# A single-core RWKV and MLP kernel: later landing times in its planner, second-batch loads held behind weight loads, and wide idle products

## The chip, the cores and the metric

The kernel runs on one core of one Trainium2 chip. The metric is device time in microseconds; lower is better. Each figure for a kernel is the median of several executions.

## The reference

The inputs are float64 in the kernel's reading (it loads pairs of 32-bit words and makes float32 of them). Per batch (4), a linear attention with decay over 768 positions, 8 heads of 48 columns:

```python
for t in range(S):
    kt, vt, rt = (k[:, :, t], v[:, :, t], r[:, :, t])
    cur = np.einsum('bhd,bhe->bhde', u[None] * kt, vt)
    y[:, :, t] = np.einsum('bhd,bhde->bhe', rt, state + cur)
    state = w[None, :, :, None] * state + np.einsum('bhd,bhe->bhde', kt, vt)
```

Its heads side by side are x (768 x 384 per batch), and then comes a gate of low rank over positions and an MLP:

```python
h = xt @ U @ V                                # U is 768 x 32, V is 32 x 768
u = x + h.transpose(0, 2, 1)
ch = np.maximum(u @ w_ch1, 0.0) @ w_ch2       # 384 -> 1536 -> 384
return (u + ch).astype(np.float32)
```

## The kernel before, in words

**Tiling.** A batch has 6 chunks of 128 positions; chunk n belongs to batch n // 6, and the chunks of the first batch are the "front" ones. For each chunk the kernel loads r, k and v (`a_load`, L630; tiles ld, or ldr, ldk and ldv) and the odd heads' v with its halves exchanged (`a_load_odd`, L661; vsw). From chunk 9 on (the second half of the second batch) r and k come as blocks of 32 rows (`a_load_blocks`, L674; bl), 32 transfers for three chunks, and DVE transposes them. A chunk's attention is done in two halves (`a_part`, L864). Each half is a run of small products on quarters of TensorE's array: pav (L824 and L830) is what the chunk gives, pab (L788 and L803) is the scores and state of the next chunk. Between the two halves a one-element copy, `seen` (L903), reads the first half's result, and the second half waits for it. After a half follow on DVE: the masking of the scores (am, L922), the state (S, L950) and, after the second half, x (L929).

**Gate and MLP.** For the first batch, x of each chunk is multiplied with U by `c_gx` (L972) into the bank `wake`; `c_g0` splits the sum (Gs). `c_x` turns x into the bank pu, `c_xu` adds the gate there and splits the result into a high and a low half (uTh, uTl). `m_1` and `m_2` are the MLP's products (p, through the helper at L344): w1 and w2 come in 12 pieces each and are also split into high and low halves (w1s, w2s). The first batch's MLP goes through its first 384 positions with half of the pieces, then through its second 384 with all, and then through the other half for the first.

**Weights.** `unit` (L492) makes a pair of steps for each of U, V and the 24 pieces: a load (L515; raw_u, raw_v, raw_w) and a conversion (L536 or L540, L562, L543, L546, then the splits at L580 and L581). No more than three pieces of w1 and w2 are under way: the load of one waits, by a dependency added by hand, for the landing of the third before it. `landing` lists these loads in their order, each with a buffer `landed_...` that stands for the landing in the plan; no tile is ever made of that buffer. The pieces' loads are taken in the order of their use.

**The planner.** All steps are first given to `Plan.op` with an engine, an estimated time, and what they read and write. `Plan.schedule` (L146) then simulates the engines and writes an order for each: at each moment it takes, among the steps that could start, the one with the smallest key (the steps' keys are the times given to `at`). The chip runs this order, each engine its own queue in turn, with semaphores only where tiles depend on each other. So an estimate changes the order and nothing else. For a DMA the plan takes a time in the queue, `LANDS` (1650 ns) and `late`; the loads of U, V and the weights have `late=LATE`, 400 ns. Where a step is ready in the plan before its data are on the chip, everything behind it on that engine's queue waits.

**The planned clock and the idle products.** The plan has a model of TensorE's clock, in windows of 3413 ns: a window runs at full speed if the window before it had work for over 0.36 of it, and at half otherwise (`clock`, L113). `pe_end` (L119) works out when a product ends and books its work. Where the plan finds TensorE idle between two given steps (`plan.wakes`, L1357), it fills the time with idle products, which nothing reads: up to the last product of `c_gx` one of the identity with itself (`waking`, L404; float32, 128 x 128, into the first 128 columns of `wake`, whose other 384 columns take `c_gx`'s sums), and later, until the first batch's first uTl is complete, `refill` (L1261), a product of V3 with V3.

## Time and profile before

| | |
|---|---|
| device time, median of 3 runs (lowest to highest) | 426.91 us (425.38 to 427.21) |
| the profiled execution's own time | 427.98 us |
| its span | 426.3 us |
| TensorE busy | 415.6 us, 98% |
| VectorE busy | 264.5 us, 62% |
| ScalarE busy | 137.3 us, 32% |
| GpSimd busy | 63.6 us, 15% |
| TensorE's granted clock, mean | 0.991 |
| DMA, mean over the span | 102 GB/s |

The span is the part of the execution that the profile shows; the profiled execution took 1.7 us more than it. Rows of the page name a line of the kernel, the engine, the operation and the tiles (out<-in). PE is TensorE, PEld its weight loads, DVE VectorE, ACT ScalarE, POOL GpSimd, and SPq and ACTq are the queues in which SyncE and ScalarE issue transfers. The slices show the whole run, 10.7 us a digit, in tenths busy and tenths of full clock:

```profile
PE   8998999999999999999999999999999999999994
DVE  6888897599999838676785466576622452113122
PEclk9998899999999999999999999999999999999999
```

TensorE is busy throughout. The first five slices hold the attention of the first batch with idle products between; from there on the MLP of each batch runs on TensorE with the attention of the next batch among it.

### The profile page before, as it was taken

What the parts mean: (1) busy time and instruction counts of PE and PEld (TensorE: products, weight loads), DVE (VectorE), ACT (ScalarE), POOL (GpSimd) and SP (SyncE); (2) the same over time, 40 slices, a digit from 0 to 9 for tenths busy, and PEclk for the clock granted to TensorE, in tenths of its full rate; (3) what the DMA queues carried; (4) which work ended last, traced back from release to release, by engine and by line L of the source; (5) the groups of instructions that cost most, each with busy time, mean ns of one, the idle gap of its engine ahead of it and who ended that gap; (6) DMA issues with size and microseconds to landing.
All of it is one profiled execution on the core that took longest, in us unless ns stands there. A gap on an engine that the chain in (4) does not pass through costs nothing.

```text
span 426.3 us, 12170 instructions
## 1 busy us (share of the span) xinstructions
PE 415.6 (98%) x5122; PEld 397.3 (93%) x5122; DVE 264.5 (62%) x598; ACT 137.3 (32%) x374; POOL 63.6 (15%) x100
## 2 busy tenths in 40 slices
PE   8998999999999999999999999999999999999994
PEld 8888899999999999999999999999999999999994
DVE  6888897599999838676785466576622452113122
ACT  2876695276541314112112221322112221111110
POOL 2654220053521003011100001101100000000000
PEclk9998899999999999999999999999999999999999
DMA  9979977697458676755477664231100420001001
GB/s 144 157 148 246 250 177 147 158 260 179 83 85 180 113 162 102 139 90 84 104 147 118 104 153 60 47 66 31 57 2 2 75 92 2 0 0 58 0 2 62
DMA packets 181951, 43.53 MB, mean 102 GB/s; under 512 B 168961, under 2 KB 180354, under 8 KB 181890
## 3 DMA queue, kind: packets, MB, share of 16 engines
q1 hardware_dynamic: 176706, 41.21, 48.2%
q10 hardware_dynamic: 5184, 1.48, 1.9%
q8 instruction: 42, 0.69, 0.7%
q14 instruction: 19, 0.16, 0.1%
HBM read 36.18 MB, written 6.49 MB: 100 GB/s over the span
## 4 chain that ended last, share of the span: by engine, by line
PE 84%; DMA 5%; SPq 5%; DVE 2%; ACT 1%; issue 1%; DVEq 0%; ACTq 0%
PE p L344 72%; SPq L655 4%; PE pav L824 4%; DMA raw_w<-in_moe_w_ch_dram 3%; PE pav L830 3%; PE pab L788 2%; PE pu L344 1%; DMA ub<-in_u_dram 1%; PE pab L803 1%; SPq L515 1%; DMA wT<-in_w_dram 1%; PE pG L995 1%; SPq L667 1%; DMA raw_v<-in_moe_V_dram 1%; DVE raw_w L543 0%
## 5 line engine op out<-in xcount | busy, mean ns | idle before, releaser
L344 PE MATMUL p<-uTh,w1s 128*128 128x384 f32 x576 | 148.2, 338 | 0.0
L1118 DVE SCALAR_TENSOR_TENSOR hl<-p,hh 128x384 fp32r<-128x384 f32 x96 | 53.0, 552 | 113.7 <-ACT hh L1117 113.5
L344 PE MATMUL p<-w2s,hh 128*128 128x384 f32 x576 | 119.3, 340 | 0.0
L1117 ACT ACTIVATE hh<-p 128x384 fp32r<-128x384 f32 x96 | 47.1, 490 | 207.2 <-PE p L344 207.2
L344 PEld LDWEIGHTS p<-uTh,w1s 128*128 128x128 f32 x576 | 103.0, 188 | 0.8
L344 PEld LDWEIGHTS p<-w2s,hh 128*128 128x128 f32 x576 | 99.9, 188 | 1.6
L344 PE MATMUL p<-uTl,w1s 128*128 128x384 f32 x288 | 96.5, 335 | 0.0
L344 PE MATMUL p<-w2s,hl 128*128 128x384 f32 x288 | 65.9, 334 | 0.0
L344 PEld LDWEIGHTS p<-uTl,w1s 128*128 128x128 f32 x288 | 54.0, 188 | 0.3 <-DVE uTl L1050 0.3
L344 PEld LDWEIGHTS p<-w2s,hl 128*128 128x128 f32 x288 | 51.4, 188 | 0.0
L824 PE MATMUL pav<-vsw,am 64*64 64x48 f32 x384 | 32.9, 224 | 0.1
L824 PEld LDWEIGHTS pav<-vsw,am 64*64 64x64 f32 x384 | 26.5, 136 | 5.5 <-issue 3.5
L788 PE MATMUL pab<-rT,kT 48*64 48x64 f32 x768 | 31.0, 226 | 0.4 <-issue 0.2
L830 PE MATMUL pav<-S,rT 48*64 48x48 f32 x704 | 31.3, 220 | 0.0
L830 PEld LDWEIGHTS pav<-S,rT 48*64 48x64 f32 x704 | 27.3, 137 | 0.0
L824 PE MATMUL pav<-ldv,am 64*64 64x48 f32 x320 | 26.5, 222 | 0.8 <-ACT seen L903 0.8
L824 PEld LDWEIGHTS pav<-ldv,am 64*64 64x64 f32 x320 | 21.5, 134 | 5.7 <-issue 4.2
L788 PEld LDWEIGHTS pab<-rT,kT 48*64 48x64 f32 x768 | 24.9, 136 | 1.7 <-issue 1.3
L698 POOL MEMSET ks<- 128x128 f32 x24 | 4.9, 205 | 137.6 <-PE pav L830 50.4
L922 DVE TENSOR_TENSOR am<-pab,mask 128x256 f32<-128x256 f32 x48 | 19.6, 416 | 6.5 <-PE pav L830 5.8
L803 PE MATMUL pab<-ldv,ks 64*48 64x48 f32 (+1 forms) x576 | 21.4, 214 | 0.0
L803 PEld LDWEIGHTS pab<-ldv,ks 64*48 64x48 f32 (+1 forms) x576 | 19.0, 130 | 0.0
(133 smaller groups left out, 500.7 us busy)
## 6 DMA issues: line engine op xcount, KB each, us to landing
raw_w<-in_moe_w_ch_dram SPq DMA_DIRECT2D x24, 384.0 KB, 5.0
out_dram<-x SPq DMA_DIRECT2D x21, 192.0 KB, 2.1
ldr<-in_r_dram SPq DMA_DIRECT2D x20, 192.0 KB, 3.4
ldk<-in_k_dram SPq DMA_DIRECT2D x20, 192.0 KB, 3.8
ldv<-in_v_dram SPq DMA_DIRECT2D x20, 192.0 KB, 3.8
bl<-in_r_dram SPq DMA_DIRECT2D x79, 48.0 KB, 2.8
bl<-in_k_dram SPq DMA_DIRECT2D x79, 48.0 KB, 2.4
vsw<-in_v_dram SPq DMA_DIRECT2D x42, 48.0 KB, 3.0
```

The lines of the kernel that those rows point to most:

```text
L344: return nc.tensor.matmul(*args, **kw)
L515: mine.append(q.dma_start(view(raw.t[p0:p0 + ap.shape[0]]), ap.bitcast(I32) if wide else ap))
L655: dma(lambda q, i=i, src=src: q.dma_start(part(i)[:, :, :D], src[b, :, c * C:(c + 1) * C, :].rearrange("h p d -> p h d")), [ts[i] if n < 4 ...
L667: dma(lambda q, i=i, s0=s0: q.dma_start(t.t[(1 - i) * C2:(2 - i) * C2], v[b, 1::2, s0:s0 + C2, :].rearrange("h p d -> p h d")), [(t, i)], ...
L698: op("POOL", 250, lambda: nc.gpsimd.memset(ks.t[:, :, D:], 0.0), [(ks, "pad")], [])
L788: return [lambda q=q, i=i: nc.tensor.matmul(pt.t[(i ^ j) * C2:(i ^ j) * C2 + C2, q * C2:(q + 1) * C2], lhsT=kT.t[rows, q, i * C2:(i + 1) * ...
L803: return nc.tensor.matmul(pt.t[j * HP:j * HP + m, SU + q * D:SU + (q + 1) * D], lhsT=ks.t[half, 2 * q + j, :m], rhs=vt()[half, 2 * q + j, ...
L824: return nc.tensor.matmul(to(q, j, i), lhsT=am[j].t[half, q, :], rhs=vsw[n].t[half, q, :] if j else vt()[half, 2 * q, :], start=(row == RO ...
L830: return nc.tensor.matmul(to(q, row, i), lhsT=rT.t[rows, q, i * C2:(i + 1) * C2], rhs=St[n, i].t[rows, q, :], start=False, stop=(row == RO ...
L922: on_dve(256, lambda e: e.tensor_tensor(am.t, abs_[n][j].t[:, :SU].rearrange("p (h t) -> p h t", h=NP), mask_.unsqueeze(1).broadcast_to([1 ...
L1117: on_act(384, lambda: nc.scalar.activation(hh.t, pt.t[:, :TB], AF.Relu), [hh], [pt])
L1118: on_dve(384, lambda e: e.scalar_tensor_tensor(hl.t, pt.t[:, :TB], 0.0, f32(hh.t), ALU.max, ALU.subtract), [hl], [pt, hh])
```

## The change

There are five edits. Loads of U and V are planned to land 2000 ns after `LANDS` and those of the weights 1500 ns, both 400 before. The loads of chunks outside the front, r, k, v and vsw, get a dependency on the landing buffer of the seventh weight load, which holds in the plan only. `pe_end` books the time that a product takes at the planned clock, where it booked its time at full clock. The idle products up to the first `c_gx` product have 512 columns: the identity, copied by ScalarE into a tile of float32r (`once`, one of the four buffers that `sel` also uses), multiplied with itself four times side by side, into the whole bank; from the first `c_gx` product to the last the narrow one stays. `c_gx` therefore starts its sum itself (`start` for the first product of chunk 0), and hands all of its products to the list `gx`, so that the first and the last can bound the two ranges of idle products. The 32-row blocks (`a_load_blocks`) keep their own dependencies.

```diff
@@ pe_end
             if note:
-                self.work[w] = self.work.get(w, 0) + part * share
+                self.work[w] = self.work.get(w, 0) + part / c * share
@@ rwkv_moe
-    LATE = 400
+    LATE = 1500
...
+    once = wbuf([128, 128], F32R, "xh", NXS, "once")
     sel = wbuf([128, 3 * 128], F32, "xh", NXS, "sel")
...
         def fn():
-            whole(bank_.t[:, :128], lhsT=ident_, rhs=ident_, start=bank_ not in awake, stop=True, skip_group_check=True)
+            whole(bank_.t[:, :128], lhsT=ident_, rhs=ident_, start=False, stop=True, skip_group_check=True)
+
+        def wide():
+            whole(bank_.t.rearrange("p (k n) -> p k n", k=4), lhsT=once.t, rhs=once.t.unsqueeze(1).broadcast_to([128, 4, 128]),
+                  start=bank_ not in awake, stop=True, skip_group_check=True)
             awake.append(bank_)
-        return fn
+        return wide, fn
@@ unit
                 dma(start, [(raw, i)] + ([landing[-1][1]] if big_one else []), [before[1]] if before else [],
-                    ap.shape[0] * runs, (8 if wide else 4) * n // runs, ns=370, late=LATE)
+                    ap.shape[0] * runs, (8 if wide else 4) * n // runs, ns=370, late=LATE if big_one else 2000)
@@ a_load
-                [ts[i] if n < 4 else (t3, i)] if n < 4 else [(ts[i], "d")], [], 1024, 192, eng=eng)
+                [ts[i] if n < 4 else (t3, i)] if n < 4 else [(ts[i], "d")], after_weights(n), 1024, 192, eng=eng)
@@ a_load_odd
-                [(t, i)], [], 256, 192, ns=610, eng="ACT" if n < 3 else "SP", dk=dk)
+                [(t, i)], after_weights(n), 256, 192, ns=610, eng="ACT" if n < 3 else "SP", dk=dk)
         vsw[n] = t
+
+    def after_weights(n):
+        return [] if front(n) else [landing[6][1]]
@@ c_gx
+        os_ = []
         for i in range(3):
-            o = pe(225, lambda i=i: whole(wk.t[:3 * R, 128 * (i + 1):128 * (i + 2)], lhsT=Uf.t[:, n].rearrange("p k r -> p (k r)"),
-                                      rhs=xs[n].t[:, 128 * i:128 * (i + 1)], start=False, stop=n == NCH - 1,
-                                      skip_group_check=True), [(wk, "g")], [Uf, xs[n]])
-        return o
+            os_.append(pe(225, lambda i=i: whole(wk.t[:3 * R, 128 * (i + 1):128 * (i + 2)], lhsT=Uf.t[:, n].rearrange("p k r -> p (k r)"),
+                                      rhs=xs[n].t[:, 128 * i:128 * (i + 1)], start=n == 0 and i == 0, stop=n == NCH - 1,
+                                      skip_group_check=True), [(wk, "g")], [Uf, xs[n]] + ([] if n or i else [once])))
+        return os_
@@ the steps and their keys
-    fill = waking(wk)
+    fill_wide, fill = waking(wk)
...
-    at(-101, lambda: ends.append(pe(230, fill, [wk], [])))
+    at(-102, lambda: on_act(128, lambda: nc.scalar.copy(once.t, ident_), [once], []))
+    at(-101, lambda: ends.append(pe(230, fill_wide, [wk], [once])))
...
-                at(max(t + (1.53 if c == NCH - 2 else 1) * per - 0.05, 36.6 + 0.01 * c), lambda n=n: gx.append(c_gx(n)))
+                at(max(t + (1.53 if c == NCH - 2 else 1) * per - 0.05, 36.6 + 0.01 * c), lambda n=n: gx.extend(c_gx(n)))
...
-    plan.wakes = [(*ends, gx[-1], fill), (*again, refill)]
+    plan.wakes = [(*ends, gx[0], fill_wide), (gx[0], gx[-1], fill), (*again, refill)]
```

## The prediction

> **What bounds the kernel now.** I read three views first: busy time by stretch, the waits of TensorE (PE), and the whole chain that ended last. The columns of the first are stretch, length, busy time of PE, PE's weight loads, VectorE (DVE), ScalarE (ACT) and GpSimd (POOL) with counts, PE clock, DMA share, GB/s; those of the waits are total, times, longest.

> ```profile
> 31.00:53.60 22.60, 20.01 (x322) 18.15 (x321) 19.20 (x42) 14.53 (x39) 7.46 (x13) 0.85 0.96 242
> 53.60:420.60 367.00, 366.65 (x4165) 352.22 (x4164) 220.41 (x482) 104.60 (x267) 39.98 (x58) 1.00 0.45 89
> ...
> PE wake L344 <- POOL ident masks.py:199: 1.7, 1, 1.7
> PE pav L824 <- DVE seen L903: 1.6, 1, 1.6
> PE pav L824 <- ACT seen L903: 0.8, 1, 0.8
> ```

> From 53.6 us to 420.6 us PE works 366.65 of 367.00 us at full clock, and the change adds and removes no work of PE there. What it can move is when the first product of the MLP (p) starts, 53.6 us. Ahead of that PE stands only for `seen`, a one-element copy between the two halves of an attention chunk, once behind DVE and once behind ACT. The chain, narrowed to that stretch, says why (start, us, what):

> ```profile
> 29.15 2.46 DMA raw_v<-in_moe_V_dram
> ...
> 32.75 0.16 DVE seen L903
> ...
> 38.80 5.85 DMA raw_w<-in_moe_w_ch_dram
> 44.67 0.56 ACT raw_w L540
> 45.26 0.15 ACT seen L903
> ...
> 53.81 2.35 PE p L344 x12
> ```

> Twice a transfer's landing releases a conversion, and `seen` sits behind that conversion in the same in-order queue. The timeline has the places, DVE's steps with the idle time ahead of each in brackets, and PE's last products of the half chunk before each:

> ```profile
> 30.59 0.22 PE L830 MATMUL pav<-S,rT 48*64 48x48 f32 x1
> ...
> 30.82 0.43 DVE L536 TENSOR_SCALAR raw_u<-raw_u 128x192 int32<-128x192 uint8 x1 [0.83 <-DMA raw_u<-in_moe_U_dram]
> 31.73 0.26 DVE L536 TENSOR_SCALAR raw_v<-raw_v 128x192 int32<-128x192 uint8 x1 [0.47 <-DMA raw_v<-in_moe_V_dram]
> ...
> 34.61 0.30 PE L803 MATMUL pab<-ldv,ks 64*64 64x48 f32 x1
> ...
> 35.48 0.36 DVE L536 TENSOR_SCALAR raw_w<-raw_w 128x384 int32<-128x384 uint8 x1 [1.11 <-DMA raw_w<-in_moe_w_ch_dram]
> 35.76 0.42 DVE L922 TENSOR_TENSOR am<-pab,mask 128x256 f32<-128x256 f32 x1
> ```

> So the planner wrote conversions of U, V and the weights into DVE's and ACT's order earlier than their data came. The third cost is the clock, by stretches of 3.41 us:

> ```profile
> 30.72:34.13 3.41, 1.85 (x53) 1.59 (x53) 2.77 (x9) 2.41 (x9) 0.93 (x4) 0.84 0.45 83
> 34.13:37.54 3.41, 3.41 (x48) 3.17 (x41) 2.29 (x7) 2.34 (x8) 0.92 (x3) 0.66 1.04 337
> 44.37:47.78 3.41, 2.58 (x41) 2.31 (x40) 2.55 (x6) 3.06 (x7) 0.21 (x1) 0.84 0.88 187
> 47.78:51.20 3.42, 3.42 (x22) 3.35 (x21) 3.42 (x5) 0.66 (x2) 2.27 (x2) 0.66 1.05 317
> ```

> Each stall of PE (busy 1.85, then 2.58 of 3.41 us) is followed by a granted clock of 0.84, then 0.66.

> **The change part by part.**

> **Landing times (400 to 1500 ns for weights, 2000 for U and V).** No instruction is added; conversions are to stand behind attention's short steps. By how much was the plan out? V's first conversion ran at 31.73 us, `seen` at 32.75, in planned order; PE's half chunk had ended at 30.81, so without the conversions `seen` could run soon after 31.0. A shift of 1.6 us carries V's behind it, so the 1.6 us of PE's wait goes. For the first weight DVE stands 1.11 us; the masking step (am) began at 35.76, though the half chunk it waits for ended at 34.91; allowing 0.2 us between the two, as above, some 0.65 us of that lies on the path (bounds 0 and 1.11). ACT's wait goes: 0.8 us. The clock loss is (0.16 + 0.34) x 3.41 twice, 3.4 us in all; fillers, and gate products hidden under attention, ran in it too, so I take half, 1.7 us (bounds 0 and 3.4). Sum: 1.6 + 0.65 + 0.8 + 1.7 = 4.75 us.

> What is late next is DVE. It is busy 19.20 of 22.60 us; its idle time, 3.4 us, plus the 0.83 us just before 31.0, is 4.2 us. If all the same DVE work stays ahead of p, p can come 4.2 us earlier at most.

> [...]

> **Second-batch loads behind weight loads.** The queue of SP, in its timeline:

> ```profile
> 30.92 2.61 SPq L515 DMA_DIRECT2D raw_w<-in_moe_w_ch_dram  x3
> 33.65 0.41 SPq L655 DMA_DIRECT2D ldr<-in_r_dram  x1
> 34.15 0.81 SPq L655 DMA_DIRECT2D ldk<-in_k_dram  x1
> 35.02 2.94 SPq L655 DMA_DIRECT2D ldv<-in_v_dram  x1
> 38.05 2.32 SPq L515 DMA_DIRECT2D raw_w<-in_moe_w_ch_dram  x3
> 40.42 1.26 SPq L667 DMA_DIRECT2D vsw<-in_v_dram  x2
> 41.79 0.54 SPq L655 DMA_DIRECT2D ldr<-in_r_dram  x1
> 42.43 1.86 SPq L655 DMA_DIRECT2D ldk<-in_k_dram  x1
> ```

> The first weight had landed by 35.48 us, yet the fourth was issued at 38.05, behind three loads of chunk 6. With those behind the seventh weight, the fourth goes out up to 2.5 us sooner. `after_weights` adds no semaphore (its buffer is never made into a tile); it changes SP's order only. I book nothing for it, since PE waits for no weight now; but it is the cover of the first edit. The tightest lead I found by comparing splits with uses is w1_5's:

> ```profile
> 65.65 1.04 POOL L581 TENSOR_TENSOR w1s<-raw_w,w1s 128x384 fp32r<-128x384 f32 x1 [8.36 <-ACT w1s L580]
> ...
> 68.52 0.51 PE L344 MATMUL p<-uTh,w1s 128*128 128x384 f32 x2
> ```

> It is ready at 66.7 and used at 68.5: 1.8 us. If p moves 4.2 us and the conversions stay, PE waits 2.4 us. With DVE's idle time squeezed out they move too. Moved back are the loads of chunks 6 to 8 and, behind them on SP, the 32-row blocks of chunk 9. From 33.65 to 37.96 and 40.42 to 44.29 SP issued 8.2 us of such loads; if it waits for landings instead, all behind comes up to 8.2 us later. What hides it:

> ```profile
> 142.03 1.13 PE pG L995 x48
> ...
> 153.87 1.32 SPq L1162 DMA_DIRECT2D out_dram<-x  x3
> ```

> Attention of the second batch must end by its pG at 142.0, and batch 0's MLP has work until about 153.9, which PE can do first: 11.8 us of cover. Cost 0, bounds 0 and 4.4 (rival C).

> **Wide idle products and their rounded identity.**

> ```profile
> 1.66 4.19 PE L344 MATMUL wake<-ident 128*128 128x128 f32 x18 [1.66 <-POOL ident masks.py:199]
> ...
> 7.68 1.50 PE L344 MATMUL wake<-ident 128*128 128x128 f32 x12
> 9.05 0.60 PE L462 MATMUL pt_tab<-ident,tw 112*128 112x112 f32 x4
> ...
> 2.03 1.28 ACT L385 ACT_TABLE_LOAD   x1 [2.03 <-issue]
> 3.42 0.51 ACT L1273 COPY sel<-ident 128x384 f32<-128x384 f32 x1
> ...
> 8.30 0.69 DVE L454 TENSOR_TENSOR tw<-tabT,wm 112x512 f32<-112x512 f32 x1
> ...
> 149.43 10.97 PE p L344 x63
> ```

> A narrow product leaves two records (six products planned, 12 shown), so it takes 0.23 us (1.38 / 6). A wide one is not in the trace; the nearest row is p, 384 columns in 10.97 / 63 = 0.174 us, so 512 columns take 0.232: equal. But the first now waits for a copy on ACT, behind the table load that ends at 3.31, where it waited for the identity at 1.66. Bounds: 0, since pt_tab waits for tw, ready at 8.99 us, whatever PE does before; and 2.2 us (3.31 + 0.51 - 1.66, at the price of the three times wider copy of sel), if all behind slips. Below zero is out: only fillers are moved. I take 0.4, nearer zero, because attention's next chunks wait for their loads anyway.

> **Busy time booked at half clock, and gx split into three operations.** Planning only; no instruction is added. The first repairs the plan's own clock, which with a later first filler would stay at half for a second window: 0.

> **The sum.** 4.75 - 0.4 = 4.35 us, capped by DVE at 4.2. From the profiled execution, 427.98 us (span 426.3 and 1.7 around it), that is 423.8; the median of the three runs is 426.91, 1.07 below it, so 422.7 us.

> **Rivals.** I call 0.5% (2.1 us) about what a measurement of this kernel can tell from no change.

> [...]

> **B, the stall is only renamed.** Later planned conversions of U and V delay the gate's operands, and p waits for Gs as it now does for `seen`; or real landings still miss the plan. For: V landed at 31.6 and Gs needs all of U. Gain 4.75 - 0.4 less the clock's 1.7 and both `seen` waits 2.4, about 0.3: 426.6.

> **C, slower: SP falls behind.** Place: the queue of SP behind weight seven. If the chunks' loads lose their 8.2 us twice, once themselves and once in the 32 block loads after them, attention of batch 1 ends 16.2 us late; it decides from 11.8 us on, so PE stands 4.4 us near 142. With only the first wait (1.6) won: 426.9 + 4.4 - 1.6 = 429.7. For: the eight rows of SP above follow each other almost without a pause. Against: what it loses is the time in which it waits for weights, and the fourth to seventh weight leave earlier for it.

> **D, more.** The clock's whole 3.4 us return and conversions slide behind p's start into the weights' leads: 4.75 + 1.7 = 6.4, no loss at the start: 420.5.

> **How the numbers follow.** Forecast (gain 3.3 to 5.4) 0.42; A 0.22; B 0.14; C 0.10; D 0.12. Faster by over 0.5% is the forecast, D and half of A: 0.65. Same is B and the other half: 0.25. Slower is C: 0.10. From D to B is 420.5 to 426.6; the bounds of filler and clock stretch it by a few tenths on either side: 420.0 to 427.0, leaving C out and a little beyond D.

> **What would show it.** Right: PE's two waits on `seen` gone; DVE's bracketed idle times at raw_u, raw_v and the first raw_w gone; clock 0.95 or more from 31 us to p's start; p starting near 49.5 us; PE still unbroken after it; the fourth weight issued by 36 us and chunk 6's loads behind the seventh. Wrong: p starting at 53 or later; PE waits on w1s or w2s splits between p's start and 70; PE idle near 90 to 145; pt_tab much behind 9.05 us, which would charge the later fillers more than 0.4.

## The result, and the profile after

| | before | after |
|---|---|---|
| device time, median of 6 runs each (lowest to highest) | 427.04 us (425.38 to 428.12) | 431.79 us (431.07 to 433.67) |
| ratio, 95% interval | | 1.0124 [1.0093, 1.0155] |
| span of the profiled execution | 426.3 us | 431.6 us |
| first product of the MLP (p) in it | 53.65 us | 58.72 us |

The change made the kernel 1.2% slower; the prediction was 422.7 us. One of the ten executions of E11 below took 2266.12 us; no ratio counts it, and E11's median is given without it. The busy time of TensorE by stretch, after (columns as in the prediction):

```profile
31.00:53.60 22.60, 20.47 (x494) 17.20 (x487) 17.14 (x43) 14.63 (x46) 4.42 (x12) 0.92 0.92 217
53.60:58.70 5.10, 5.10 (x39) 4.69 (x38) 5.01 (x11) 4.05 (x10) 0.00 (x0) 1.00 1.01 223
58.70:425.70 367.00, 366.44 (x4165) 352.26 (x4163) 223.38 (x488) 101.25 (x259) 42.45 (x60) 1.00 0.44 88
```

From p on TensorE is as busy as before: 366.44 of 367.00 us, against 366.65. Of the 5.3 us by which the two spans differ, 5.1 lie ahead of p. (Both profiles show long executions of their kernels: 427.98 us, and 433.67, the longest of its six.) TensorE's waits ahead of p, after (total, times, longest):

```profile
PE pab L811 <- issue: 2.5, 2, 2.2
PE pav L832 <- issue: 1.9, 2, 1.3
PE pab L796 <- ACT tab L469: 0.5, 1, 0.5
PE pab L811 <- DVE ks L707: 0.4, 1, 0.4
PE pav L832 <- DVE am L930: 0.2, 1, 0.2
```

The waits on `seen` are gone, as forecast. In their place stands 4.4 us of "issue", a wait without any releaser. The timeline has its four places, all inside a half chunk:

```profile
19.67 0.43 PE L811 MATMUL pab<-ld,ks 64*48 64x48 f32 x10 [0.31 <-issue]
...
26.74 0.25 PE L811 MATMUL pab<-ld,ks 64*64 64x48 f32 x1 [2.20 <-issue]
...
33.75 0.25 PE L832 MATMUL pav<-ld,am 64*64 64x48 f32 x1 [0.59 <-issue]
...
39.68 0.25 PE L832 MATMUL pav<-vsw,am 64*64 64x48 f32 x1 [1.28 <-issue]
```

The second thing is the start. ScalarE and its queue, after:

```profile
0.81 1.28 ACT L385 ACT_TABLE_LOAD   x1 [0.81 <-PEq L1389]
1.65 0.46 ACTq L660 DMA_DIRECT2D ld<-in_k_dram  x1
...
2.21 0.29 ACT L1279 CAST once<-ident 128x128 fp32r<-128x128 f32 x1
...
9.44 2.28 ACTq L672 DMA_DIRECT2D vsw<-in_v_dram  x2
11.76 0.48 ACT L469 COPY tab<-pt_tab 128x384 f32<-128x384 f32 x1 [7.71 <-DMA vsw<-in_v_dram]
```

The copy to `once` brings ScalarE's table load forward, from 2.03 to 0.81 us, and the k load of chunk 0 now stands behind that (issued at 1.65, before at 0.81). Every later load on that queue slips, and `tab`, which the first chunk needs and whose input pt_tab is there from 10.42 us, is copied at 11.76, behind two loads of vsw.

### The profile page after: what moved, and what is told of

Same layout as the page of the kernel before. It is cut to its first block, busy times and chain, and to the rows that moved or that the text cites. A ratio compares the mean times of both kernels' runs of the same rounds, so it can differ in the third digit from the quotient of the medians.

```text
span 431.6 us, 12073 instructions
## 1 busy us (share of the span) xinstructions
PE 417.0 (97%) x5074; PEld 394.0 (91%) x5074; DVE 267.2 (62%) x604; ACT 132.9 (31%) x359; POOL 60.1 (14%) x98
## 4 chain that ended last, share of the span: by engine, by line
PE 93%; DMA 2%; issue 1%; ACT 1%; DVE 1%; ACTq 0%
PE p L344 72%; PE pav L832 5%; PE pav L838 4%; PE wake L344 3%; PE pab L796 2%; PE pab L811 2%; PE pu L344 2%; DMA vsw<-in_v_dram 1%; PE ptr L757 1%; PE ptk L757 1%; PE pG L1004 1%; DMA ld<-in_k_dram 1%; PE ph L344 0%; DVE ks L707 0%; ACT raw_w L567 0%
## 5 line engine op out<-in xcount | busy, mean ns | idle before, releaser
L344 PE MATMUL p<-uTh,w1s 128*128 128x384 f32 x576 | 148.3, 338 | 0.0
L344 PE MATMUL p<-w2s,hh 128*128 128x384 f32 x576 | 119.4, 341 | 0.0
L344 PEld LDWEIGHTS p<-uTh,w1s 128*128 128x128 f32 x576 | 103.1, 188 | 0.8
L344 PEld LDWEIGHTS p<-w2s,hh 128*128 128x128 f32 x576 | 99.9, 188 | 1.6
L344 PE MATMUL p<-uTl,w1s 128*128 128x384 f32 x288 | 96.7, 336 | 0.0
L344 PE MATMUL p<-w2s,hl 128*128 128x384 f32 x288 | 66.0, 335 | 0.0
L344 PEld LDWEIGHTS p<-uTl,w1s 128*128 128x128 f32 x288 | 54.1, 188 | 0.3 <-DVE uTl L1059 0.3
L344 PEld LDWEIGHTS p<-w2s,hl 128*128 128x128 f32 x288 | 51.5, 188 | 0.0
L344 PE MATMUL wake<-once 128*128 128x512 f32 x50 | 17.7, 494 | 2.6 <-ACT once L1279 2.6
```

The source lines that it names most:

```text
L344: return nc.tensor.matmul(*args, **kw)
```

## The parts of the change, one by one

**Theories.** I: the idle products cost, by the later start and by the stalls on issue; the rest is free or gains. L: later landing times and moved loads cost, the idle products don't. The four kernels:

- E1: before, with `pe_end`, the wide products, `once` and the split of `c_gx` alone.
- E2: before, with the two landing times alone.
- E3: before, with `after_weights` alone.
- E4: E2 and E3 together.

E1 and E4 together are the whole change.

> The kernel before with only the idle products' edits (wide products, the rounded identity copied by ScalarE, gx in three operations, busy time booked at half clock); landing times and loads as before. Theory I (idle products: the copy put first on ScalarE delays the first chunk's k and the table tab, and TensorE's stream then stands without a semaphore): slower by 3 to 6 us, 430 to 433 us, first p product at 57 to 59 us, over 2 us of 'issue' ahead of pav and pab, tab at 11.5 us or later. Theory L (landing times and the moved loads): within 1 us of before, 426 to 428 us, first p product at 53 to 54.5 us, tab near 9.7 us.

> The kernel before with only the later landing times. Theory I: faster by 2 to 4 us, 423 to 425 us, since both waits for seen go and nothing holds up the start; first p product at 50 to 52 us. Theory L: no gain or slower, 427 to 431 us, because conversions planned later hold up the gate; first p product at 53.5 us or later.

> The kernel before with only the second-batch loads behind weight loads. Theory I: within 1.5 us of before (425.5 to 428.5 us), the first p product within 1 us of 53.6. Theory L: slower by 2 us or more, since the 32-row blocks slip ahead of the weights on SyncE's queue in place of the chunk loads.

> The change without the idle products' edits (narrow products as before, no copy). Theory I: faster than before by 2 to 4 us, 423 to 425 us, first p product at 50 to 52 us. Theory L: as slow as the change, 430 to 433 us, first p product at 57 us or later.

| | median | ratio to before, 95% interval | p in its profile | idle on issue ahead of p |
|---|---|---|---|---|
| E1 wide idle products | 431.66 | 1.0073 [1.0025, 1.0121] | 58.00 | 5.7 |
| E2 landing times | 427.41 | 1.002 [0.9998, 1.0043] | 50.78 | 0.3 |
| E3 held loads | 427.14 | 0.9999 [0.9969, 1.003] | 53.11 | 0 |
| E4 both of these | 428.38 | 1.0047 [1.0022, 1.0072] | 53.53 | 0.9 |

(The kernel before in the same job: 426.79 us.) E1 and E3 came out as theory I expected. E2 gained nothing, as theory L had it for the time (p is early, as theory I had it), and E4 lies between the two. The ratios of E1 and E4 make up the whole: 0.73% and 0.47% against 1.24%. E1's ratio is less than its median says (4.9 us, or 1.1%), since one of its five executions took 427.82 us; its interval is wide, some 1 to 5 us. So the idle products cost, and so does the rest, by a means that theory I did not have. Both parts needed a closer look.

## Why idle products cost: the supply of instructions

E1's stalls, from its timeline:

```profile
26.50 0.25 PE L808 MATMUL pab<-ld,ks 64*64 64x48 f32 x1 [2.20 <-issue]
...
33.35 0.25 PE L829 MATMUL pav<-ld,am 64*64 64x48 f32 x1 [1.99 <-issue]
...
38.74 0.27 PE L793 MATMUL pab<-rT,kT 48*64 48x64 f32 x1 [0.54 <-issue]
...
43.74 0.20 PE L835 MATMUL pav<-S,rT 48*64 48x48 f32 x1 [0.98 <-issue]
```

From one to the next are 126, 126 and 127 records of products, and from one to the next in the changed kernel 127, 126 and 126. The page has queues of instructions (packets, MB, share):

```profile
q8 instruction: 42, 0.69, 0.7%
q14 instruction: 19, 0.16, 0.1%
```

0.69 MB in 42 transfers is 16.4 KB each. Between two such stalls the trace of the changed kernel holds 256 instructions of TensorE: the 127, 126 and 126 products, 126 weight loads each time, and 3, 4 and 4 semaphore instructions. Over 256 instructions 16.4 KB is 64 bytes each. Asked for 0.1 us of the changed kernel, just as its longest stall begins (24.54 us), the DMA view shows one of them:

```profile
DMA packets 116, 0.04 MB, mean 383 GB/s; under 512 B 115, under 2 KB 115, under 8 KB 115
...
q8 instruction: 1, 0.02, 59.1%
```

The traces bear the edges out. Number the records of products from the first one of each trace: the stalls end at records 220, 347, 473 and 599 in the changed kernel and at 347, 473, 599 and 726 in E1. In all fifteen traces of this case every wait on issue of over 0.15 us ahead of p ends at one of these numbers, give or take one, or, in E8 below, at 853, the next: in the kernel before, at 220 (0.2 us, and 0.7 in a second execution), in E6 at 346, 473, 599 and 727. At none of these six edges of any trace does TensorE take the edge's record earlier than 2.2 us after the transfer began. At the second edge the transfer began 2.7 us ahead of the record in the kernel before (18.74 and 21.46 us), while some 76 records were still to start; in the changed kernel (24.44 us) none was.

The rival **T**: the loss is the late start alone. Four kernels tell the two apart. E5 issues each wide product as two, which gives the edges nearly their old places:

```diff
-            whole(bank_.t.rearrange("p (k n) -> p k n", k=4), lhsT=once.t, rhs=once.t.unsqueeze(1).broadcast_to([128, 4, 128]),
-                  start=bank_ not in awake, stop=True, skip_group_check=True)
+            for j in range(2):
+                whole(bank_.t[:, 256 * j:256 * (j + 1)].rearrange("p (k n) -> p k n", k=2), lhsT=once.t,
+                      rhs=once.t.unsqueeze(1).broadcast_to([128, 2, 128]),
+                      start=bank_ not in awake, stop=True, skip_group_check=True)
```

> The changed kernel with each wide idle product issued as two of 256 columns; the plan and every order are those of the changed kernel, only the number of TensorE's instructions differs. Theory S (supply): TensorE's instructions arrive in blocks of 128 products with their weight loads (a product of float32 counts twice), and the changed kernel stands where a block's edge falls deep in a half chunk that directly follows another. Two products for one put the edges back to within 8 records of where the kernel before has them. S expects: TensorE's idle time with no releaser (issue) between 15 and 58 us falls from 4.4 us to under 1.5 us, p starts 2 to 4 us sooner than in the changed kernel, time 428 to 430. Theory T (start): the whole loss is the later start of chunk 0, because ScalarE copies the identity ahead of its loads; the plan's fixed idle products never let it be made up. T expects no gain: 431 to 432.5.

E6 copies the identity on VectorE:

```diff
-    at(-102, lambda: on_act(128, lambda: nc.scalar.copy(once.t, ident_), [once], []))
+    at(-102, lambda: op("DVE", dve(128), lambda: nc.vector.tensor_copy(out=once.t, in_=ident_), [once], []))
```

> The changed kernel with the rounded identity copied by VectorE instead of ScalarE, so that ScalarE's first loads go out ahead of its table load as before. Both theories expect tab, the table that the first chunk waits for, near 10 us instead of 11.8. T expects the whole loss back: 426.5 to 428. S expects only the start back, with the stalls on issue still 3 to 5 us in all: 429.5 to 431.

E7 is both:

> Both edits, the products in two and the copy on VectorE. S: no stalls over 1.5 us in all and no late start, so near the change without its idle products (428.4): 426.5 to 429. T: as the copy on VectorE alone, 426.5 to 428, and equal to it within 0.5.

E8 is the kernel before with fewer idle products:

```diff
+    unbooked = [14]
...
         def fn():
+            unbooked[0] -= 1
+            if unbooked[0] >= 0:
+                return
             whole(bank_.t[:, :128], lhsT=ident_, rhs=ident_, start=bank_ not in awake, stop=True, skip_group_check=True)
```

> The kernel before with its first 14 idle products left out, all of them before 6 us, when TensorE has nothing else to do: the output is the same, only idle work is missing. This moves every later block edge by 28 records, to 42, 30, 60 and 40 records into half chunks of 64. S expects new stalls on issue of 2 to 5 us in all between 15 and 50 us and a time 1 to 4 us over the kernel before: 428 to 431. T expects no difference: 426 to 427.5.

| | median | ratio to before, 95% interval | p | idle on issue | tab copied at |
|---|---|---|---|---|---|
| E5 products in two | 428.46 | 1.0036 [1.0012, 1.006] | 53.1 | 0 | 11.91 |
| E6 copy on VectorE | 430.06 | 1.0085 [1.0055, 1.0115] | 55.8 | 4.5 | 10.48 |
| E7 both | 428.09 | 1.0039 [1.002, 1.0057] | 52.8 | 0 | 10.65 |
| E8 before, 14 idle products fewer | 427.62 | 1.0011 [0.9988, 1.0034] | 53.5 | 2.7 | 10.78 |

(Before in this job: 426.77 us.) E5 is the clearest. Its plan and its streamed columns are those of the changed kernel, and only the number of TensorE's instructions differs. All waits of TensorE in its profile:

```profile
PE wake L344 <- ACT once L1281: 2.6, 1, 2.6
PE pu L344 <- DVE Gs L996: 1.5, 1, 1.5
PE pav L834 <- DVE am L932: 1.1, 1, 1.1
PE pab L813 <- DVE ks L709: 0.4, 1, 0.4
PE pab L798 <- ACT tab L471: 0.3, 1, 0.3
```

No "issue" is left, and the time falls from 431.79 to 428.46 us, 3.3 us, as S said; T said no gain. The ratios, each taken beside the kernel before, say the same: 1.0124 and 1.0036, with intervals well apart. E6 took most of the late start away (`tab` at 10.48; 11.76 with the change, 9.69 before) and left the stalls; its median is 1.7 us below the changed kernel's, though the two intervals overlap, so a gain is not shown. Both together give 3.7 us, not 5: E5 has the late start and E7 has little of it, and they differ by 0.4 us, their ratios not at all (1.0036 and 1.0039). So without the stalls the late start costs nothing that these runs can tell; what it costs with them is open.

E8 shows the stalls in the kernel before, by leaving idle work out:

```profile
18.55 0.20 PE L808 MATMUL pab<-ld,ks 64*64 64x48 f32 x1 [0.20 <-issue]
...
24.98 0.20 PE L829 MATMUL pav<-vsw,am 64*64 64x48 f32 x1 [1.65 <-issue]
...
34.23 0.25 PE L835 MATMUL pav<-S,rT 48*64 48x48 f32 x1 [0.23 <-issue]
...
39.52 0.25 PE L808 MATMUL pab<-ldv,ks 64*64 64x48 f32 x1 [0.42 <-issue]
```

In the trace they stand 42, 28, 56 and 35 records into their half chunks; 42, 30, 60 and 40 were expected, from 128 records to a block, where the traces above have 126 or 127. With one more of 0.18 us they are 2.7 us, within S's 2 to 5. The count has one more edge between the second and the third, 10 records into a half chunk, and no stall is seen there. But the time, 427.62 us, is 0.85 above before, under S's range (428 to 431), just over T's (426 to 427.5), and no change lies within its interval. Its profile has 0.8 us of waits for VectorE ahead of p, where the second profile of the kernel before (E9, below) has 2.2; that the stalls ran in place of such waits fits this, but is not shown.

## Why the landing times gained nothing

Next the kernel before was profiled a second time (E9), and the landing times were taken apart: weights alone (E10), U and V alone (E11), and all about half as late (E12).

```diff
E10
-    LATE = 400
+    LATE = 1500
-                    ap.shape[0] * runs, (8 if wide else 4) * n // runs, ns=370, late=LATE)
+                    ap.shape[0] * runs, (8 if wide else 4) * n // runs, ns=370, late=LATE if big_one else 400)
E11: LATE = 400, "else 2000"
E12: LATE = 900, "else 1000"
```

> The kernel before once more, for a second profile. If the half clock of the first profile (two stretches, some 3 us) is an event of that execution and no property of the kernel, this one shows a granted clock of 0.95 or more in all stretches from 15 to 53 us, p starting 1 to 3 us sooner than 53.65, and a time of 425 to 426.5; the two waits on seen (2.4 us) stay. If it belongs to the kernel, p starts near 53.6 again and the clock falls below 0.9 in at least one stretch.

> The kernel before with the weights' planned landing at 1500 and that of U and V left at 400. Theory R (the waits are renamed): ScalarE's conversion ahead of seen goes, but V's ahead of DVE's seen stays, and the freed time turns into waits on Gs or am; time 426 to 427.5. Theory G (the later weights gain, the later U and V give it back): 424.5 to 426, with p 0.8 us or more sooner than in the second profile of the kernel before.

> The kernel before with the planned landing of U and V at 2000 and that of the weights left at 400. R: the wait on seen behind DVE goes, and waits on Gs, Uf or uTl of about its size come; time 426 to 427.5. G: slower than the kernel before, 427.5 to 429, with waits on Gs and Uf over 1.5 us in all.

> The kernel before with 900 for the weights and 1000 for U and V. If the size of the landing times matters, and the best lies between 400 and those of the change, this is the fastest of all: 424 to 426. R: 426 to 428, like the two ends.

| | median | ratio to before, 95% interval | p |
|---|---|---|---|
| E9 before, one execution | 425.29 | | 51.5 |
| E10 weights later | 427.09 | 0.9988 [0.9958, 1.0017] | 50.2 |
| E11 U and V later | 428.98 | 1.0049 [1.0028, 1.0071] | 52.9 |
| E12 half as late | 428.17 | 1.0043 [1.0008, 1.0079] | 54.5 |

(Before in this job: 427.05 us.) E9 bears on the forecast's main term. The waits of TensorE ahead of p, and the stretches in which the first profile had its half clock:

```profile
PE pab L788 <- DVE rT L758: 1.0, 2, 0.5
PE pu L344 <- DVE Gs L985: 1.0, 1, 1.0
PE pab L788 <- issue: 0.7, 1, 0.7
PE wake L344 <- ACT Uf L586: 0.3, 1, 0.3
PE pav L824 <- DVE seen L903: 0.2, 1, 0.2
```

```profile
34.13:37.54 3.41, 2.62 (x48) 2.16 (x48) 2.57 (x9) 2.48 (x8) 0.79 (x3) 1.00 1.06 289
...
47.78:51.20 3.42, 2.40 (x16) 2.09 (x15) 3.36 (x6) 2.54 (x7) 2.33 (x2) 1.00 1.09 316
```

The same kernel, another execution: 0.2 us on `seen` where the first had 2.4, and a clock of 1.00 where it had 0.66. I had expected the two waits to stay; they went too, and the first execution's 427.98 us lies 2.7 above this one. So the prediction's waits and clock are not fixed properties of the kernel. Neither are they singular: waits on `seen` of 0.9 us stand in E3 and 1.3 in E10, and of the 95 executions of the kernel before that were run beside the experiments, 30 had a mean granted clock of 0.994 or less (0.991 in the first profile, 0.999 in E9), with a median of 428.18 us, against 426.47 for the other 65. E9, at 425.29, is itself a short one. In it the chain through VectorE, rT and Gs, is what TensorE waits for most ahead of p.

Into that chain the change puts later conversions. E11's longest waits:

```profile
PE pu L344 <- DVE Gs L985: 1.7, 1, 1.7
PE pab L788 <- DVE rT L758: 0.9, 1, 0.9
...
PE wake L344 <- ACT Uf L586: 0.4, 1, 0.4
```

Later U and V alone cost 0.5%. The wait on Gs grew from 1.0 to 1.7 us, with Uf it is 2.1, over G's 1.5, and the time is at the end of G's range (427.5 to 429). The profile shows the shortest of E11's executions (427.06 us), so only a part of the loss: the four at a mean clock of 0.996 or more took 427.06 to 427.41 us, the five at 0.995 or less 428.98 to 430.6. So beside the longer waits the clock fell in more of them; the record shows the two together, and which comes first was not tried. Later weights alone do not gain measurably, where G expected 424.5 to 426. E10's p is 1.3 us sooner than E9's, as G had it, but 1.6 us of waits on uTl follow in p itself, which the table's p does not show. So G is right about U and V and wrong about the weights. E2 has both and measured 1.002; its interval overlaps E11's, so whether the later weights give some of it back is open. E12, the one value tried between, is no better: 428.17, outside both forecasts, and 2.6 us of waits on Gs in its profile.

Do U and V explain what E7 still loses (1.0039)? E13 is E7 with U and V at 400:

```diff
-                    ap.shape[0] * runs, (8 if wide else 4) * n // runs, ns=370, late=LATE if big_one else 2000)
+                    ap.shape[0] * runs, (8 if wide else 4) * n // runs, ns=370, late=LATE if big_one else 400)
```

> The changed kernel with the products in two, the copy on VectorE, and U and V's planned landing back at 400 ns; what is left of the change are the weights' landing times, the held loads, the busy time in the plan's clock and wide idle products without their two costs. If U and V's later conversions are what is left of the loss (later U and V alone: ratio 1.005), it is level with the kernel before: 425.5 to 427.3, waits on Gs under 1 us. If the held loads or the wide products cost something of their own, it stays at the 428 of both edits.

It measured 426.24 us, ratio 0.9996 [0.9974, 1.0018], before 426.52. TensorE's waits ahead of p:

```profile
PE pav L834 <- DVE seen L913: 0.9, 1, 0.9
PE pab L798 <- DVE rT L768: 0.4, 1, 0.4
PE p L344 <- DVE uTl L1061: 0.2, 1, 0.2
PE pv L344 <- PE ptr L759: 0.2, 1, 0.2
```

No wait on Gs, and level with before. So the ratio's way from 1.0124 is: 1.0039 without the stalls and most of the late start, 0.9996 with U and V early as well; the two steps' intervals don't touch. No kernel tried here is shown to be faster than the one before.

## Why the prediction was wrong, step by step

- **What bounds the kernel** (p's start; TensorE unbroken behind it): right, in both kernels.
- **Landing times, 4.2 us of gain**: this step failed. The `seen` waits went, as forecast, but the gain was read from one execution whose 2.4 us of such waits and two half-clock stretches a second one did not have, and the time that later conversions of U and V cost at Gs was put at nothing in the sum. Measured alone: ratio 1.002 [0.9998, 1.0043], no gain. The sign was there: the profiled execution was the slowest of all that the prediction had, 1.07 us over the median, and the forecast took that 1.07 off at the end without asking which of its waits were the 1.07. Of the rivals, B named this mechanism (V's and U's later conversions delay the gate): right in kind for E11, whose waits on Gs grew.
- **Clock, 1.7 us of that sum**: the loss of the first profile was missing from the second, and 30 of the 95 executions of the kernel before had a mean clock of 0.994 or less. The change did not remove it either: its profile has 0.92 from 31.00 to 53.60 us, where 0.95 or more was the sign, with two stretches at 0.51 (from 27.30 and from 40.96 us), each behind a stall (2.20 and 1.28 us). What halves the clock these runs don't show (last section).
- **Second-batch loads, 0**: right, 0.9999 alone (interval 0.3% either way). One detail was not: the fourth weight was issued at 36.79 us, not by 36, since the 32-row blocks, which keep their own dependencies, took SP's turn from 33.31. Rival C did not come: the profile after shows no wait of TensorE between 58 and 150 us.
- **Wide idle products, 0.4 us, bounds 0 and 2.2**: this step failed most. Alone they cost 0.73% (1.0025 to 1.0121, some 1 to 5 us). The price of a wide product's time was right (0.23 us from one to the next); its count of instructions was not priced at all, and with the stalls gone (E5) the loss falls from 1.24% to 0.36%. The copy was priced as a delay of the first filler alone. It also moved ScalarE's table load ahead of its first DMA, and `tab` came 2.1 us later than before. "Attention's next chunks wait for their loads anyway" overlooked that these loads are issued by the queue that the copy delays; pt_tab at 9.87, not 9.05, was the sign named. What this late start costs by itself, these runs can't tell. The stalls on issue were in none of the rivals. That a narrow product leaves two records was noted, and used only for its duration.
- **`pe_end` and the split of `c_gx`, 0**: not tried apart; E13 contains them and is level.
- **The range** ended at 427.0 and left out C, the only slower case. C had another place (SP) and another price (429.7) than what came; no case had the supply of instructions.

## What to carry to other kernels

An idle product is also so many instructions: changing its shape moves the places where the next block of instructions must have come (here 126 or 127 products apart, with stalls of up to 2.20 us), so look for waits named "issue" and for their spacing before judging a filler by its streaming time. A wait that a profile shows once should be looked for in a second execution before its removal is booked, above all where that execution is the longest at hand. A copy put at the front of an engine that also issues loads has to be priced by what it moves in that queue (here `tab`, 2.1 us later), not by its duration (0.29 us), and then by whether anything waits for that.

## What the runs showed of the hardware

In these runs a gap did not decide the clock by its length alone, or by the busy time in a stretch around it. The changed kernel and E1 each stood 2.20 us in the same stretch, busy 1.21 of 3.41 us. The changed kernel, that stretch and the next:

```profile
23.89:27.30 3.41, 1.21 (x65) 1.03 (x57) 1.01 (x3) 1.30 (x6) 0.00 (x0) 0.99 0.68 136
27.30:30.72 3.42, 3.42 (x12) 2.67 (x12) 2.31 (x5) 2.35 (x10) 2.73 (x4) 0.51 1.00 204
```

And E1:

```profile
23.89:27.30 3.41, 1.21 (x50) 1.03 (x42) 0.98 (x4) 1.05 (x5) 0.17 (x1) 1.00 0.73 144
27.30:30.72 3.42, 3.42 (x80) 2.66 (x77) 2.90 (x7) 2.62 (x11) 2.80 (x5) 1.00 0.91 192
```

The first fell to 0.51, the second stayed at 1.00. Read at 23.83:27.24 and 27.24:30.66 the changed kernel's clock is 1.00 and 0.50, and so it is at 37.48:40.90 and 40.90:44.31: between the first chunk and p half clock came twice, each time for 3.41 us, the starts 13.65 us (four times that) apart, and the 2.20 us gap lies wholly inside the 3.41 us ahead of the first. E1 has no half clock here (1.00 in every such stretch from 20.48 to 47.78 us), so its rows don't show how its gap lies to such stretches, and whether that makes the difference stays open. The gap's length does not settle it at other places either: the kernel before fell to 0.50 (46.67:50.09) behind a wait of 0.83 us, and E1 stayed at 1.00 (34.13:37.54) behind one of 1.99. The plan's model of the clock is the kernel's own and was not put to a test; by busy time alone it does not fit the kernel before, busy 2.58 of 3.41 us (43.26:46.67) just ahead of that 0.50. Open as well is what decides when the next block is asked for: between the start of its transfer and the edge stood some 76 records in one kernel and none in another.
